# Keys in runs, scores at a step, and the banks of P·V, relu and output dealt out anew: a fused window attention and MLP kernel

## The chip, the cores and the metric

The kernel runs on one core of one Trainium2 chip. The metric is the device time of one execution in microseconds (us). TensorE is called PE, VectorE DVE, ScalarE ACT, GpSimd POOL and SyncE SP; SP only issues DMAs here.

## The reference

Sliding window attention for 8 batches of 8 heads, 576 positions and 64 numbers a head, and then an MLP without residual on the 4608 rows of 512 that come out of it:

```python
scores = scale * np.matmul(q, k.transpose(0, 1, 3, 2))
mask = np.abs(pos[:, None] - pos[None, :]) <= 32
attn = softmax(np.where(mask, scores, -1e9))           # with + 1e-9 in the divisor
x = np.matmul(attn, v)  ->  transposed to (B*S, H*D) = (4608, 512)
r = np.maximum(x @ w_in, 0.0)                          # w_in 512 x 2048
out = (s * (r * r) + b) @ w_out                        # w_out 2048 x 512, s and b scalars
```

All inputs and the output are float32. The kernel computes its matmuls in bf16.

## The kernel before

The 4608 rows are 36 tiles of 128 tokens. A tile is two units of 64 queries; with a window of 32, each unit needs 128 keys, which overlap by half, so a tile needs 192 keys (32 before it to 32 behind it). All eight heads of a tile are done together, as four pairs of heads.

**Order.** Nothing is looped over in the finished program. Each operation is added as a node with an engine, a cost, a key and the names it reads and writes; `_Plan.order` then simulates the engines with these costs and takes, on whichever engine comes free, the ready node with the smallest key. The outcome is a fixed instruction list for each engine, with semaphore waits between them. Keys count tokens: the FFN of a tile has the key of its tokens (`t0`), its attention is drawn ahead by `akey(j) = 128*j - min(640, 500 + 50*j)`. An engine may be given as a set, such as `("act", "dve")`; the planner then chooses. Nodes marked `small` use the PE array as quarters of 64 x 64, and the planner tries to keep them together (`HOLD`, `DEFER`), since a switch costs time. `fill` puts idle matmuls on PE ahead of a node for which the plan waits, in the stages named by `FILL`, in number by `FILL_SHARE` and `FILL_NS`.

**Attention.** Loads of q, k and v go through SP's queue in order (`load`, L506), each gated by the tile five before it. POOL casts them to bf16 (`cast_kq`, `cast_v`). From tile 12 on, DMA transposes q and k; up to 11, PE does it through the bank `TPF`. k is loaded as two neighbouring token rows in one partition, so that after the transposition the even and the odd keys lie in two halves, 1 KB apart; `scores` (L798) reads them in the order of tokens:

```python
kk = KQT["k"][...][rows, :, pr, p0 % 128:p0 % 128 + (x1 - x0) // 2].rearrange("q t p -> q p t")
```

The first four tiles take keys and queries from `TURN` (`kwt`, `qwt`), which the first batch's raw rows are turned into on PE (`turn_raw`), and there the keys lie in runs. Scores fill two PSUM banks `SC`. DVE adds the mask and takes the maximum (L810), ACT exponentiates (L818), POOL divides (L831). From tile 6 on a DMA transposes the probabilities into `PTS` (L845).

**P·V.** `VE[j]` holds the 128 rows of v that begin 32 before the tile, so unit 0 has its keys in `VE[j]` and unit 1 has half in `VE[j]`, half in `VE[j+1]`. Up to `NOLD` (6), unit 1 has its own copy `VO` in key order (`make_vo`, two casts of 64 rows), and `av_one` (L869) does 16 matmuls in full-array mode into the bank `AV`. From `NOLD` on, `av` (L886, L892) does 24 matmuls in quarter mode, into `AV` and a second bank, `PTPF`; ACT copies the second bank (`HALF`, L901), and DVE adds the two into `XT` (L903). Tiles 0 to 2 (`LIGHT`) go another way: `attend_light` computes the scores a second time in transposed form and does P·V in two steps of 16 and 8 matmuls (L733).

**FFN.** The first 8 tiles run alone, the other 28 in pairs of 256 tokens. `s1` (L992) multiplies `XT` by w_in into a relu bank, ACT takes the relu (L1001), DVE squares it (L1020), `s2` (L1040) multiplies by w_out, and DVE scales and adds a constant row into `OUTS` (L1054), from which SP stores. Of the eight PSUM banks, the relu banks are `HT[0]`, `HT[1]` and, from token 1408 on, `TPF`; the out bank is `OUTP`, and for tiles 0 to 4 `PTPF` in turn with it (`ONE`). The last three pairs turn through four banks.

**Weights.** w_in and w_out come in four blocks each (`load_w`), as float32 into free parts of `GT` (`SLOT`), and are cast on POOL. The third and the fourth w_out block reuse the slots of the first and the second.

Of the kernel before, what the change touches and what calls it, by code (L numbers as in the profile page):

```python
# [6 lines left out]
F32 = mybir.dt.float32  # L7
# [7 lines left out]
DM = H * D  # L15
# [12 lines left out]
FILL, FILL_MIN, FILL_SHARE, FILL_NS = ("attn", "ffn", "sums"), 300.0, 0.7, 115.0  # L28
# [34 lines left out]
class _Plan:  # L63
# [202 lines left out]
    last = {}  # L266
# [4 lines left out]
def bass_sliding_window_symmetric__then__act_starrelu_kernel(  # L271
# [19 lines left out]
    WSET = {"i": ("pool",), "o": ("pool",)}  # L291
# [3 lines left out]
    SLOT = dict(i0=0, i1=1, i2=2, i3=3, o0=2, o1=3, o2=2, o3=3)  # L295
# [5 lines left out]
    NWHOLE = 0  # L301
    AVK, NOLD, ONE, NVO = 5, 6, 5, 2
# [11 lines left out]
    def OSET(j):  # L314
        return ("act", "dve")

    with ExitStack() as es:
# [31 lines left out]
        OUTS = [sb((128, DM), F32, "outs") for _ in range(NO)]  # L349
# [28 lines left out]
        AVF = ps((128, 512), F32, "av")  # L378
        AV = AVF[:, :].rearrange("p (a b) -> p a b", b=128)
# [66 lines left out]
        def fill(e, stage, n):  # L446
            for _ in range(n):
                if stage == "sums":
                    r = e.matmul(OUTP[:, 0:256], lhsT=NIL[:, :], rhs=ONES[:, :], start=False,
                                 stop=False)  # L450
                else:
                    r = e.matmul((HT[1] if stage == "attn" else OUTP)[:, 0:256],
                                 lhsT=ONES[:, 0:128], rhs=ONES[:, :], start=True, stop=True)
# [17 lines left out]
        def load_w(which, c):  # L471
            s_ = SLOT[which + str(c)]
            w32 = GT[:, 4 + 2 * s_:6 + 2 * s_, :, :].rearrange("p a b c -> p (a b c)").bitcast(
                F32).rearrange("p (g c) -> p g c", g=4)
            src = (w_in[:, :, 512 * c:512 * c + 512] if which == "i"
                   else w_out[:, 4 * c:4 * c + 4, :])
            lastload[0] = add("sp", lambda e: [e.dma_start(w32, src)], 500, -LEAD - 900,
                              writes=[("W32", s_, g) for g in range(4)], dsem=f"dw{s_}",
                              dtime=2850, behind=lastload[0], ndesc=512)
# [136 lines left out]
        def make_vo(j):  # L616
            s_, a, b_ = j % NVO, j % NVE, (j + 1) % NVE
            if j < LIGHT or j >= NOLD:
                return
            for r0, x in ((64, j), (0, j + 1)):  # L620
                sl = x % (NL + 1)
                move(OSET(j), {"act": 620.0, "dve": 425.0},
                     VO[s_][r0:r0 + 64, :], V32[sl][r0:r0 + 64, :],
                     akey(j) - 10, [("V32", sl)] + ([("V32", 0, "lo")] if x == 0 else []),
                     [("VO", s_, r0)])
# [30 lines left out]
        def attend_light(j):  # L656
# [69 lines left out]
            ve, vb = j % NVE, (j + 1) % NVE  # L726
            steps = [[(1, vb, 0, 64), (0, ve, 0, 128)], [(1, ve, 64, 128)]]
            before = None
            for i, step in enumerate(steps):
                def av(e, step=step, i=i):  # L730
                    for u, vt, k0, k1 in step:
                        for y in range(8):
                            r = e.matmul(AVF[64 * u:64 * u + 64, 64 * y:64 * y + 64],  # L733
                                         lhsT=PTS[ptb][k0:k1, y, 64 * u:64 * u + 64],
                                         rhs=VE[vt][k0:k1, 64 * y:64 * y + 64],
                                         start=(i == 0 and y == 0),
                                         stop=(y == 7 and (i == 1 or u == 0)))
                    return r

                n = add("pe", av, 300 * len(step), key + 3, reads=pts + [("VE", ve), ("VE", vb)],  # L740
                        writes=["AV"])
                n.hard, before = before, n
            turned[j] = n
# [29 lines left out]
        def attend(j):  # L773
# [12 lines left out]
            def scores(e):  # L786
                for pr in range(NPAIR):
                    for u, x0, x1, y0 in ((0, 0, 128, 0), (1, 0, 64, 128), (1, 64, 128, 64)):
                        for hh in range(2):
                            if whole:  # L790
                                qq, kk = qs(j, pr, hh, 64 * u, 64 * u + 64), keys(j, pr, hh, y0, y0 + x1 - x0)
                            else:
                                rows, p0 = slice(64 * hh, 64 * hh + 64), 64 * (j % 2) + y0 // 2
                                qq = KQT["q"][c % NKT["q"]][rows, j % 2, pr, 64 * u:64 * u + 64]
                                kk = KQT["k"][(c + p0 // 128) % NKT["k"]][
                                    rows, :, pr, p0 % 128:p0 % 128 + (x1 - x0) // 2].rearrange(
                                    "q t p -> q p t")
                            r = e.matmul(SC[hh][64 * u:64 * u + 64, pr, x0:x1], lhsT=qq, rhs=kk,  # L798
                                         start=True, stop=True)
                return r  # L800
# [81 lines left out]
            def av(e):  # L882
                for pr in range(NPAIR):
                    for hh in range(2):
                        d0, y = 128 * pr + 64 * hh, 2 * pr + hh
                        e.matmul(PTPF[64 * hh:64 * hh + 64, 128 * pr:128 * pr + 128],  # L886
# [12 lines left out]
            add("pe", av, 265, key + AVK, reads=pts + [("VE", ve), ("VE", (j + 1) % NVE)], writes=["AV", "PTP"]).mode = "small"  # L899
            hb = j % 2  # L900
            add("act", lambda e: e.copy(HALF[hb][:, :], PTPF[:, :]), 620, key + AVK, reads=["PTP"],  # L901
# [69 lines left out]
        for m, nt in enumerate(TILES):  # L971
# [8 lines left out]
            for f0 in range(0, 16, fg):  # L980
                hb, rb = hcnt[0] % (3 if KQDMA < NT and t0 >= 128 * KQDMA else 2), rcnt[0] % NR1
# [43 lines left out]
            for sub in range(nt // 128):  # L1025
                r0 = t0 + 128 * sub
                end = r0 + 128 == T
                for c0, cn in ((0, 256), (256, 256)) if end else ((0, 512),):
# [4 lines left out]
                                 )[ocnt[0] % (4 if last else 2 if t0 < 128 * ONE else 1)]  # L1033
# [17 lines left out]
                    if not cvec_done[0]:  # L1051
# [5 lines left out]
                        60 + 1.35 * cn, key - 2000, reads=[ores, "CVEC", "SCB"], writes=[("OUTS", ob)])  # L1057
# [63 lines left out]
```

## Time and profile before

| | before |
|---|---|
| median of 3 runs | 331.92 us (330.61 to 332.28) |
| the profiled execution | 331.01 us, span 329.3 us |
| granted TensorE clock, mean | 0.995 |
| busy: PE, DVE, ACT, POOL | 314.1, 219.6, 215.9, 163.1 us |
| scores L798 / P·V L886 + L892 | 768 + 24 / 240 + 480 matmuls |
| idle fill matmuls L452 | 55, the last group at 24.10 us |

The profile comes from one execution. Busy time is the union of an engine's instructions; matmuls overlap, so the mean length of one is longer than the distance between two. In timelines each row is a start, a length, an engine, a line, an operation with output and inputs, its shape and count, and in brackets the idle time ahead of it.

### The profile page before, as it was taken

What the parts mean: (1) busy time and instruction counts of PE and PEld (TensorE: products, weight loads), DVE (VectorE), ACT (ScalarE), POOL (GpSimd) and SP (SyncE); (2) the same over time, 40 slices, a digit from 0 to 9 for tenths busy, and PEclk for the clock granted to TensorE, in tenths of its full rate; (3) what the DMA queues carried; (4) which work ended last, traced back from release to release, by engine and by line L of the source; (5) the groups of instructions that cost most, each with busy time, mean ns of one, the idle gap of its engine ahead of it and who ended that gap; (6) DMA issues with size and microseconds to landing.
All of it is one profiled execution on the core that took longest, in us unless ns stands there. A gap on an engine that the chain in (4) does not pass through costs nothing.

```text
span 329.3 us, 10479 instructions
## 1 busy us (share of the span) xinstructions
PE 314.1 (95%) x4119; PEld 220.5 (67%) x4169; DVE 219.6 (67%) x869; ACT 215.9 (66%) x731; POOL 163.1 (50%) x220
## 2 busy tenths in 40 slices
PE   6889999999999999999999999999999999999996
PEld 4557966677776766766666676666767676656664
DVE  2446797888876887777667667767866767634332
ACT  5415745587877787697777777786877779723230
POOL 5576688565763656535454547464654532220000
PEclk9799999999999999999999999999999999999999
DMA  5999969939999999979999999999999652221011
GB/s 164 353 293 286 311 228 237 238 106 233 167 196 212 267 203 218 218 152 230 198 225 181 197 221 227 200 184 220 185 217 198 137 124 67 64 66 64 34 55 73
DMA packets 155297, 61.30 MB, mean 186 GB/s; under 512 B 129392, under 2 KB 146160, under 8 KB 155248
## 3 DMA queue, kind: packets, MB, share of 16 engines
q1 hardware_dynamic: 154960, 60.64, 87.1%
q8 instruction: 32, 0.52, 0.7%
q14 instruction: 17, 0.14, 0.2%
q10 hardware_dynamic: 288, 0.00, 0.0%
HBM read 37.03 MB, written 9.44 MB: 141 GB/s over the span
## 4 chain that ended last, share of the span: by engine, by line
PE 79%; DMA 9%; DVE 3%; POOL 3%; issue 3%; SPq 2%; POOLq 0%
PE outp L1040 26%; PE ht L992 25%; PE tp L992 8%; PE sc L798 5%; DMA gt<-in_q_dram 3%; DMA v<-in_v_dram 2%; PE sc L1040 2%; DMA pts<-p 2%; DMA r32k<-in_k_dram 2%; PE ptp L886 2%; PE ptp L1040 2%; PE av L1040 2%; DVE gt L1020 1%; SPq L506 1%; POOL p L831 1%
## 5 line engine op out<-in xcount | busy, mean ns | idle before, releaser
L1020 DVE TENSOR_TENSOR gt<-r 128x512 bf16<-128x512 bf16 x144 | 82.4, 574 | 54.8 <-ACT r L1001 53.5
L831 POOL TENSOR_TENSOR p<-p,rc 128x512 bf16<-128x512 bf16 x65 | 72.6, 1136 | 90.0 <-DVE rc L826 90.0
L1040 PE MATMUL outp<-wout,gt 128*128 128x512 bf16 (+1 forms) x436 | 111.9, 375 | 5.1 <-issue 4.1
L992 PE MATMUL ht<-xt,win 128*128 128x256 bf16 (+1 forms) x1152 | 114.1, 249 | 0.8 <-DVE xt L903 0.4
L818 ACT ACTIVATE p<-ss,mx 128x128 bf16<-128x128 f32 x264 | 103.0, 392 | 17.8 <-DVE mx L810 17.5
L992 PEld LDWEIGHTS ht<-xt,win 128*128 128x128 bf16 x1152 | 91.9, 98 | 24.8 <-DVE xt L903 1.2
L1001 ACT ACTIVATE r<-ht 128x512 bf16<-128x512 f32 x112 | 66.2, 592 | 44.4 <-PE ht L992 43.6
L810 DVE CUSTOM_DVE_ANT_0 ss<-sc,mask 128x128 f32<-128x128 f32 x264 | 62.1, 282 | 12.6 <-PE sc L798 12.3
L1040 PEld LDWEIGHTS outp<-wout,gt 128*128 128x128 bf16 x480 | 43.4, 98 | 33.8 <-issue 0.4
L818 ACT ACTIVATION_READ_ACCUMULATOR p<-ss,mx 128x1 f32 x264 | 50.0, 189 | 0.0
L992 PE MATMUL tp<-xt,win 128*128 128x256 bf16 x256 | 33.2, 273 | 0.0
L992 PEld LDWEIGHTS tp<-xt,win 128*128 128x128 bf16 x256 | 25.0, 98 | 8.0
L526 POOL CAST ve<-v 128x512 bf16<-128x512 f32 x37 | 24.0, 653 | 11.7 <-PE av L892 9.7
L1001 ACT ACTIVATE r<-tp 128x512 bf16<-128x512 f32 x32 | 18.9, 592 | 12.3 <-PE tp L992 11.1
L526 POOL CAST kn<-r32k 128x512 bf16<-128x512 f32 x34 | 21.5, 659 | 7.3 <-DMA r32k<-in_k_dram 7.3
L1054 DVE SCALAR_TENSOR_TENSOR outs<-outp,scb,cvec 128x512 f32<-128x512 f32 (+1 forms) x30 | 22.1, 736 | 3.4 <-PE outp L1040 3.4
L901 ACT COPY half<-ptp 128x512 f32<-128x512 f32 x30 | 17.4, 579 | 10.5 <-PE av L892 10.5
L526 POOL CAST qn<-r32q 128x512 bf16<-128x512 f32 x32 | 20.1, 628 | 4.2 <-DMA r32q<-in_q_dram 4.2
L798 PE MATMUL sc<-kt,qt 64*64 64x64 bf16 (+1 forms) x768 | 22.1, 243 | 0.0
L810 DVE DVE_READ_ACCUMULATOR2_ANT mx<- 128x1 f32 x264 | 21.3, 81 | 0.0
L903 DVE TENSOR_TENSOR xt<-av,half 128x512 bf16<-128x512 f32 x30 | 20.5, 683 | 1.1 <-ACT half L901 1.1
L798 PEld LDWEIGHTS sc<-kt,qt 64*64 64x64 bf16 x768 | 17.5, 107 | 4.7 <-issue 3.6
(133 smaller groups left out, 244.2 us busy)
## 6 DMA issues: line engine op xcount, KB each, us to landing
out_dram<-outs SPq DMA_DIRECT2D x35, 256.0 KB, 3.1
v<-in_v_dram SPq DMA_DIRECT2D x28, 256.0 KB, 5.5
r32q<-in_q_dram SPq DMA_DIRECT2D x28, 256.0 KB, 4.9
r32k<-in_k_dram SPq DMA_DIRECT2D x9, 512.0 KB, 5.0
gt<-in_moe_w_in_dram SPq DMA_DIRECT2D x4, 1024.0 KB, 10.0
gt<-in_moe_w_out_dram SPq DMA_DIRECT2D x4, 1024.0 KB, 6.9
v<-in_v_dram SPq DMA_DIRECT2D x8, 192.0 KB, 4.7
r32k<-in_k_dram SPq DMA_DIRECT2D x3, 448.0 KB, 4.5
```

The costliest lines, as they stand in the source:

```text
L526: return e.tensor_copy(dst, src)
L798: r = e.matmul(SC[hh][64 * u:64 * u + 64, pr, x0:x1], lhsT=qq, rhs=kk, start=True, stop=True)
L810: lambda e, ss=ss, x=x, y=y, pr=pr, hh=hh: e.tensor_tensor_reduce(out=SS[ss][:, x, :], in0=SC[hh][:, pr, :], in1=MASK[kind][:, :], scale=- ...
L818: lambda e, ss=ss, x=x, y=y: e.activation(P[pb][:, y, :], SS[ss][:, x, :], AF.Exp, bias=MX[mb][:, y:y + 1], scale=-1.0, accum_out=SM[mb][: ...
L831: return e.tensor_tensor(P[pb][:, y0:y0 + 4, :], P[pb][:, y0:y0 + 4, :], RC[mb][:, y0:y0 + 4].unsqueeze(2).broadcast_to([128, 4, 128]), AL ...
L901: add("act", lambda e: e.copy(HALF[hb][:, :], PTPF[:, :]), 620, key + AVK, reads=["PTP"], writes=[("HALF", hb)])
L903: add("dve", lambda e: e.tensor_tensor(XT[:, :, 128 * (j % NX):128 * (j % NX) + 128], AV[:, :, :], HALF[hb][:, :].rearrange("p (a b) -> p ...
L992: r = e.matmul(hbank[:, nt * f:nt * f + nt], lhsT=WIN[:, kc, 128 * ft:128 * ft + 128], rhs=XT[:, kc, x0:x0 + nt], start=(kc == 0), stop=(k ...
L1001: return e.activation(R1[rb][:, :], hbank[:, :], AF.Relu, bias=0.0, scale=1.0)
L1020: return e.tensor_tensor(d, r, r, ALU.mult)
L1040: r = e.matmul(op_[:, 0:cn], lhsT=GT[:, g_, fc, :], rhs=WOUT[:, fc, c0:c0 + cn], start=(fc == 0), stop=(fc == 15))
L1054: add("dve", lambda e, ob=ob, op_=op_, c0=c0, cn=cn: e.scalar_tensor_tensor(OUTS[ob][:, 0:cn], op_[:, 0:cn], SCB[:, 0:1], CVEC[:, c0:c0 + cn],
```

## The change

- The keys of tiles 4 and on are read in two runs (even tokens, odd tokens), and the score matmul writes its columns at a step of two, so that the scores lie in token order as before.
- The second bank of P·V is `TPF` instead of `PTPF`. The relu banks are two throughout, and `OUTP` and `PTPF` take turns as out banks throughout.
- `AVK` goes from 5 to 384: P·V of tile j and the copy of its second bank get the key of the scores of tile j + 3.
- `NOLD` goes from 6 to 12, and the light tiles use `VO` too: their P·V is one step of 16 matmuls. The casts into `VO` may run on POOL for tiles 0 to 2.
- The third w_out block is staged in the four output buffers (now one tensor), the fourth in the third's old slot; w_out is cast on ACT or POOL.
- Fillers are 512 columns wide, planned as half of waits over 400 ns, and not in the stage "ffn". The planner is given longer times for the first raw loads.

```diff
-FILL, FILL_MIN, FILL_SHARE, FILL_NS = ("attn", "ffn", "sums"), 300.0, 0.7, 115.0
+FILL, FILL_MIN, FILL_SHARE, FILL_NS = ("attn", "sums"), 400.0, 0.5, 220.0
...
-    WSET = {"i": ("pool",), "o": ("pool",)}
+    WSET = {"i": ("pool",), "o": ("act", "pool")}
...
-    SLOT = dict(i0=0, i1=1, i2=2, i3=3, o0=2, o1=3, o2=2, o3=3)
+    SLOT = dict(i0=0, i1=1, i2=2, i3=3, o0=2, o1=3, o2=4, o3=2)
...
-    NWHOLE = 0
-    AVK, NOLD, ONE, NVO = 5, 6, 5, 2
+    NWHOLE, SECOND = 0, True
+    AVK, NOLD, ONE, NVO = 384, 12, 11, 2
...
     def OSET(j):
-        return ("act", "dve")
+        return ANY if j < LIGHT else ("act", "dve")
...
-        OUTS = [sb((128, DM), F32, "outs") for _ in range(NO)]
+        OUTA = sb((128, NO, DM), F32, "outs")
+        OUTS = [OUTA[:, i, :] for i in range(NO)]
...
+        AV2, AV2N = (TPF, "TP") if SECOND else (PTPF, "PTP")
...
-        add("pe", lambda e: fill(e, "attn", 14), 2990, K0, reads=["ONES", "NIL"]).tag = "attn"
+        add("pe", lambda e: fill(e, "attn", 7), 2990, K0, reads=["ONES", "NIL"]).tag = "attn"
...
-            w32 = GT[:, 4 + 2 * s_:6 + 2 * s_, :, :].rearrange("p a b c -> p (a b c)").bitcast(
-                F32).rearrange("p (g c) -> p g c", g=4)
+            w32 = OUTA if s_ == 4 else GT[:, 4 + 2 * s_:6 + 2 * s_, :, :].rearrange(
+                "p a b c -> p (a b c)").bitcast(F32).rearrange("p (g c) -> p g c", g=4)
...
-                              dsem=f"dr{x}{half}", dtime=1500, behind=lastload[0], ndesc=128)
+                              dsem=f"dr{x}{half}", dtime=1900 if x + str(half) != "K0" else 2650, behind=lastload[0], ndesc=128)
...
-            if j < LIGHT or j >= NOLD:
+            if j >= NOLD:
                 return
...
-            steps = [[(1, vb, 0, 64), (0, ve, 0, 128)], [(1, ve, 64, 128)]]
...
+            def av(e):
+                for u, vt in ((0, VE[ve]), (1, VO[vo])):
+                    for y in range(8):
+                        r = e.matmul(AVF[64 * u:64 * u + 64, 64 * y:64 * y + 64],
+                                     lhsT=PTS[ptb][:, y, 64 * u:64 * u + 64],
+                                     rhs=vt[:, 64 * y:64 * y + 64], start=(y == 0), stop=(y == 7))
+                return r
...
+                            dst = SC[hh][64 * u:64 * u + 64, pr, x0:x1]
...
                                 kk = KQT["k"][(c + p0 // 128) % NKT["k"]][
-                                    rows, :, pr, p0 % 128:p0 % 128 + (x1 - x0) // 2].rearrange(
-                                    "q t p -> q p t")
-                            r = e.matmul(SC[hh][64 * u:64 * u + 64, pr, x0:x1], lhsT=qq, rhs=kk,
-                                         start=True, stop=True)
+                                    rows, :, pr, p0 % 128:p0 % 128 + (x1 - x0) // 2]
+                                dst = dst.rearrange("q (p t) -> q t p", t=2)
+                            r = e.matmul(dst, lhsT=qq, rhs=kk, start=True, stop=True)
...
-                        e.matmul(PTPF[64 * hh:64 * hh + 64, 128 * pr:128 * pr + 128],
+                        e.matmul(AV2[64 * hh:64 * hh + 64, 128 * pr:128 * pr + 128],
...
-                hb, rb = hcnt[0] % (3 if KQDMA < NT and t0 >= 128 * KQDMA else 2), rcnt[0] % NR1
+                hb, rb = hcnt[0] % (3 if not SECOND and t0 >= 128 * KQDMA else 2), rcnt[0] % NR1
...
-                                 )[ocnt[0] % (4 if last else 2 if t0 < 128 * ONE else 1)]
+                                 )[ocnt[0] % (4 if last else 2 if SECOND or t0 < 128 * ONE else 1)]
...
-                        60 + 1.35 * cn, key - 2000, reads=[ores, "CVEC", "SCB"], writes=[("OUTS", ob)])
+                        60 + 1.35 * cn, key - 2000, reads=[ores, "CVEC", "SCB"], writes=[("OUTS", ob), ("W32", 4, ob)])
```

More of the change, by code (lines that the diff above doesn't have):

```diff
@@ L621, in make_vo @@
                 sl = x % (NL + 1)
-                move(OSET(j), {"act": 620.0, "dve": 425.0},
+                move(OSET(j), {"act": 620.0, "dve": 425.0, "pool": 640.0},
                      VO[s_][r0:r0 + 64, :], V32[sl][r0:r0 + 64, :],
@@ L725, in attend_light @@
             pts = [("PTS", ptb, y) for y in range(8)]
-            ve, vb = j % NVE, (j + 1) % NVE
-            steps = [[(1, vb, 0, 64), (0, ve, 0, 128)], [(1, ve, 64, 128)]]
[L728 to L743, printed above, removed]
+            ve = j % NVE
+            vo = j % NVO
+            def av(e):
[5 more added lines that the diff above has]
+                return r
+            turned[j] = add("pe", av, 700, key + 3,
+                            reads=pts + [("VE", ve), ("VO", vo, 0), ("VO", vo, 64)], writes=["AV"])
             def rows(e):
```

13 lines of the change are left out of this document (6 added, 7 removed).

## The prediction

> **What bounds the kernel now.** I read the page first: the busy table, the row of 40 slices, the chain that ended last.
>
> ```profile
> span 329.3 us, 10479 instructions
> ...
> PE 314.1 (95%) x4119; PEld 220.5 (67%) x4169; DVE 219.6 (67%) x869; ACT 215.9 (66%) x731; POOL 163.1 (50%) x220
> ...
> PE   6889999999999999999999999999999999999996
> ...
> PE 79%; DMA 9%; DVE 3%; POOL 3%; issue 3%; SPq 2%; POOLq 0%
> ```
>
> TensorE (PE) is busy in 95% of the span and carries 79% of the chain; no other engine passes 67%. Then the windows, one for each stage: the light start, the time until w_out is in, the stage with two relu banks, the stage with three, the end.
>
> ```profile
> 14.90:26.48 11.58, 10.18 (x205) 6.35 (x205) 4.65 (x12) 2.37 (x5) 7.96 (x14) 1.00 0.98 325
> 26.48:60.00 33.52, 32.42 (x539) 25.59 (x537) 27.07 (x75) 18.65 (x55) 24.36 (x37) 1.00 1.00 254
> 60.00:115.00 55.00, 53.69 (x835) 38.97 (x847) 43.62 (x192) 42.42 (x159) 32.52 (x43) 1.00 1.01 203
> 135.00:282.00 147.00, 143.47 (x1783) 100.31 (x1804) 105.05 (x457) 112.72 (x400) 75.22 (x93) 1.00 0.98 183
> 282.00:329.30 47.30, 44.13 (x372) 28.60 (x376) 18.11 (x49) 15.62 (x37) 2.90 (x3) 1.00 0.19 62
> ```
>
> The columns are length, then busy time with its count for PE, PEld, DVE, ACT and POOL, then the granted clock (1.00 in all of them), DMA share and GB/s. From 26.48 us, where the first tile's FFN begins, PE lacks 1.10, 1.31 and 3.53 us, which is 2 to 3%. Part of that is not idleness: where a group of four matmuls shows three records, the missing one is counted as a 0.16 us gap (a row below). So from 26.5 us on the time is the sum of what PE is given to do. An edit that takes matmul time away shortens the kernel by that much, and an edit that only removes waits of other engines brings next to nothing.
>
> **The change part by part.** *Scores.* All 32 full-form tiles from 4 on read keys at L798 in steps of 1 KB (two interleaved token rows); tile 3 reads the same shapes in runs, from the turned first batch.
>
> ```profile
> L798 PE MATMUL sc<-kt,qt 64*64 64x64 bf16 x512 | 22.0, 222 | 0.0
> L798 PE MATMUL sc<-kt,qt 64*64 64x128 bf16 x256 | 21.8, 284 | 0.0
> ...
> L798 PE MATMUL sc<-kwt,qwt 64*64 64x64 bf16 x16 | 0.4, 195 | 0.0
> L798 PE MATMUL sc<-kwt,qwt 64*64 64x128 bf16 x8 | 0.4, 222 | 0.0
> ```
>
> One 128-column matmul takes 284 ns with the step and 222 in runs, one of 64 columns 222 against 195: 62 and 27 ns more. Of a whole block the timeline gives the cost, as the distance to the next group on PE:
>
> ```profile
> 31.99 0.45 PE L798 MATMUL sc<-kwt,qwt 64*64 64x128 bf16 x24
> 32.37 1.01 PE L992 MATMUL ht<-xt,win 128*128 128x128 bf16 x15
> ...
> 62.19 0.69 PE L798 MATMUL sc<-kt,qt 64*64 64x128 bf16 x24
> 62.81 1.04 PE L1040 MATMUL outp<-wout,gt 128*128 128x512 bf16 x4
> ```
>
> 24 matmuls take 0.38 us in runs and 0.62 with the step. After the change all 32 blocks read runs: 32 x 0.24 = 7.7 us off, if the new step of two fp32 elements in the score bank is free. No row of the trace shows a matmul that writes with a step. Its bounds: the write can't be better than in runs, so 0.38 us is the floor; the nearest row above is the stepped read, 0.62, where nothing is gained. I take 0.38, because the rows that differ here differ in the read alone, and no row shows PE held by its writes. [...]
>
> *P·V of tiles 12 to 35, tied to the scores three tiles on.* These blocks switch PE into quarter-array mode and back, as the scores do.
>
> ```profile
> 122.24 0.24 PE L886 MATMUL ptp<-pts,ve 64*64 64x128 bf16 x2
> ...
> 183.25 0.24 PE L886 MATMUL ptp<-pts,ve 64*64 64x128 bf16 x2
> ...
> 183.50 0.28 PE L798 MATMUL sc<-kt,qt 64*64 64x128 bf16 x1
> ...
> 184.35 0.81 PE L1040 MATMUL outp<-wout,gt 128*128 128x512 bf16 x3 [0.16 <-issue]
> ...
> 197.38 0.69 PE L798 MATMUL sc<-kt,qt 64*64 64x128 bf16 x24
> 198.22 0.81 PE L1040 MATMUL outp<-wout,gt 128*128 128x512 bf16 x3 [0.16 <-issue]
> 198.97 0.24 PE L886 MATMUL ptp<-pts,ve 64*64 64x128 bf16 x2
> ...
> 199.34 0.82 PE L1040 MATMUL outp<-wout,gt 128*128 128x512 bf16 x3
> ...
> 245.59 0.24 PE L886 MATMUL ptp<-pts,ve 64*64 64x128 bf16 x2
> ```
>
> The record left out before 184.35 and 198.22 is one of about 0.22 us (four last 1.04 in a row above, three 0.81), so those groups begin at 184.13 and 198.00. Together the pair takes 184.13 - 183.25 = 0.88 us. Apart they take 0.62 + 0.37 = 0.99, and each stands behind a switch of some 0.10 (198.00 + 4 x 0.22 = 198.87, and the block begins at 198.97): 0.2 us more. In the trace the P·V of six tiles from 12 on stands apart (the first at 122.24, the last before the scores run out at 245.59), and after it one more of the last three does, because tiles 33 to 35 find no scores three tiles on: five pairs saved, 1.0 us. The key also puts the copy of the second bank on ScalarE (L901) later, behind relus. What covers that: the key lets P·V run 256 tokens before its FFN, two tiles, and 36 tiles take some 300 us, 8.3 each. If the cover failed, that copy and the add (0.58 and 0.68 us, below) would be late on PE.
>
> *Tiles 6 to 11 by the older form.* They take the one-bank form of P·V (L869), which tiles 3 to 5 show:
>
> ```profile
> 59.09 0.32 PE L869 MATMUL av<-pts,ve 128*64 128x64 bf16 x8
> ...
> 59.47 0.62 PE L642 MATMUL tp<-ident,kn 128*128 128x128 bf16 x8
> ```
>
> That is 59.47 - 59.09 = 0.38 us in full-array mode, against 0.25 (183.50 - 183.25) for the quarter form where it is paired and 0.37 plus a switch of 0.10 where it isn't. With four of the six paired: 4 x 0.13 - 2 x 0.09 = +0.3 us. Each also needs two casts into VO on ScalarE or VectorE, and loses the copy of the second bank:
>
> ```profile
> L901 ACT COPY half<-ptp 128x512 f32<-128x512 f32 x30 | 17.4, 579 | 10.5 <-PE av L892 10.5
> L531 ACT CAST vo<-v 64x512 bf16<-64x512 f32 x2 | 1.2, 614 | 0.5 <-PE av L869 0.4
> ...
> L903 DVE TENSOR_TENSOR xt<-av,half 128x512 bf16<-128x512 f32 x30 | 20.5, 683 | 1.1 <-ACT half L901 1.1
> L526 DVE CAST vo<-v 64x512 bf16<-64x512 f32 x4 | 3.2, 806 | 1.0 <-DMA v<-in_v_dram 1.0
> ```
>
> Twelve casts at the mean of 614 and 806, less six copies of 579: 8.5 - 3.5 = 5.0 us more on two engines that have 11.4 and 12.6 us free of 55 in that stage. Hidden, it costs nothing; behind each cast wait exponentials (ACT) or squares (DVE) in line, and these feed PE. Bounds 0 and 5.0; I take 1.0, near the end that PE's 2% of idleness in the stage speaks for.
>
> *Light tiles 0 to 2.* Their P·V goes from 24 matmuls in two steps, the second waiting for the first, to 16 of the form of L869; six VO casts are added on whichever engine is free (ACT 2.37 and DVE 4.65 us of 11.58 busy).
>
> ```profile
> 22.08 0.80 PE L733 MATMUL av<-ve,pts 64*64 64x64 bf16 x16
> 22.81 0.39 PE L691 MATMUL ptp<-maskt,ident 128*128 128x512 bf16 x1
> ...
> 23.61 0.41 PE L733 MATMUL av<-ve,pts 64*64 64x64 bf16 x8
> 23.95 0.22 PE L704 MATMUL sc<-ident,m 128*16 128x128 bf16 x1
> 24.10 0.77 PE L452 MATMUL ht<-ones 128*128 128x256 bf16 x4
> ...
> 26.48 1.07 PE L992 MATMUL ht<-xt,win 128*128 128x128 bf16 x16
> ```
>
> 0.73 + 0.34 = 1.07 us become 0.38: 0.69 off each. For tiles 1 and 2, after 26.48, PE is full: 1.4 us off. For tile 0 the second step stood behind the next tile's scores, so its result came at 23.95 and could come at 22.08 + 0.38 = 22.46; PE's own work falls by 0.69 and the first FFN could begin up to 1.5 us earlier. I take 1.0.
>
> *Banks.* Relu banks go from three to two, out banks from one to two. The stage from 60 to 115 us already runs on two relu banks and one out bank, with PE 97.6% busy, like the stage with three (97.6%): nothing either way. The stepped write fills the same places, so readers of the scores see no change.
>
> *w_out, fillers, dtimes.* The third w_out load no longer waits on SP's queue for POOL's casts, and those casts may go to ScalarE:
>
> ```profile
> SPq L477 <- POOL wout L526: 8.8, 2, 5.4
> ```
>
> Loads of q, k and v behind it come up to 5.4 us earlier. But PE lacks only 1.10 us between 26.48 and 60, covered by FFN work on the first tiles: at most 1.1 is to be had, and a cast in front of an exponential can lose as much; I take nothing. The fillers (L452) stand in predicted waits before 26.48 us; shorter ones could at most give back those like the 0.77 us at 24.10 or lose that in a colder clock; nothing again. The new dtimes only move the plan of the first casts.
>
> The sum: -7.7 - 1.0 + 0.3 + 1.0 - 1.4 - 1.0 = -9.8 us. The profiled execution took 331.01 us with 329.3 of span; 331.0 - 9.8 = 321.2. The median of the runs shown is 0.9 above the profiled one, so I forecast **322.1 us**, and 319.5 to 325 if its mechanism holds.
>
> **The rivals.** *The step only moves from the read to the write.* The write costs what the read cost, the blocks stay at 0.62 us, and the rest remains: -9.8 + 7.7 = -2.1, 329.8 us. For it: the halved rate of the read at a step shows that this engine's streams can be held by a step. Against it: no row shows PE waiting on its bank. [...]
>
> *Slower: the stepped write costs more than the stepped read.* Its place is the 32 blocks at L798. If the write adds to the old block once more what the step added to the read, a block takes 0.62 + 0.24 = 0.86 us: 32 x 0.24 - 2.1 = +5.6, 337.5 us. It decides from (2.1 + 1.7) / 32 = 0.12 us above the old block, at 0.74 us. For it: all four quarters of the array write at once, two of them into one bank. Against it: a read at 62 ns extra for 128 columns is a rate of one half, and nothing suggests a quarter.
>
> *The other engines become the bound in tiles 6 to 11.* All 5.0 us of added casts come out on PE instead of 1.0: 326.1 us. For it:
>
> ```profile
> 70.00:80.00 10.00, 9.79 (x161) 7.27 (x161) 9.41 (x45) 7.78 (x33) 6.26 (x8) 1.00 0.61 146
> ```
>
> DVE is busy 9.41 of 10 us there. Against it: PE is full in that same window.
>
> **How the numbers follow.** Forecast 0.52; other engines bound 0.10; step moved to the write 0.22; slower 0.16. About 0.5% (1.7 us) is what a measurement of this kernel tells from no change. The first two are faster; the third, at 329.8, lies just past that bound, and I give 0.13 of it to faster and 0.09 to the same. Faster 0.75, same 0.09, slower 0.16. The range 319.5 to 331.0 holds the first three cases and leaves out the slower one and a few hundredths below.
>
> **What would show it.** In the new profile: the L798 forms at 222 and 195 ns, a block at 0.38 us before a full-array group, P·V of tile j right beside the scores of tile j + 3, L733 with 16 matmuls in 0.4 us, the first FFN near 25.5 us, and PE still above 97% in the middle stages. Wrong: L798 at 284 ns or more, or PE's share falling in 60 to 115 us while DVE or ACT rises above 90%.

## The result, and the profile after

| | before | changed |
|---|---|---|
| median, first comparison | 332.1 us (4 runs) | 327.57 us (4 runs), ratio 0.986 [0.982, 0.991] |
| median, once more beside the experiments | 331.17 us (11 runs) | 325.64 us (4 runs), ratio 0.982 [0.980, 0.985] |
| profiled execution | 331.01 us, span 329.3 | 326.15 us, span 324.4 |

The change makes the kernel 4.5 to 5.5 us faster. The forecast was 9.8 us, to 322.1: the direction and the outer range (319.5 to 331.0) hold, but less than half of the gain came, in the first comparison. The experiments below compare by ratios to the kernel before, each on the chip that it ran on; 0.1% is 0.33 us.

The page of the changed kernel, its busy table, slices and chain:

```profile
span 324.4 us, 10296 instructions
...
PE 308.5 (95%) x4013; PEld 215.3 (66%) x4064; DVE 218.3 (67%) x878; ACT 223.0 (69%) x742; POOL 157.3 (49%) x212
...
PE   6689989999999999999999999999999999999996
...
PE 78%; DMA 10%; DVE 3%; POOL 3%; SPq 2%; issue 2%; ACT 1%; DVEq 0%; POOLq 0%
```

The same stages as before (length, then busy time of PE, PEld, DVE, ACT, POOL, granted clock, DMA share, GB/s):

```profile
14.90:26.48 11.58, 10.39 (x224) 6.25 (x222) 7.55 (x19) 3.70 (x8) 8.10 (x14) 1.00 0.98 331
26.48:60.00 33.52, 31.32 (x513) 24.44 (x516) 25.89 (x79) 21.62 (x60) 20.76 (x31) 1.00 1.10 269
60.00:115.00 55.00, 53.33 (x774) 38.76 (x779) 45.69 (x207) 46.28 (x172) 33.48 (x41) 1.00 1.05 201
135.00:282.00 147.00, 144.89 (x1810) 101.07 (x1833) 102.82 (x463) 114.53 (x403) 72.34 (x90) 1.00 0.98 184
```

PE is still the bound: it lacks 1.67 and 2.11 us in the two long stages, 1.31 and 3.53 before. What is new is idleness between 26.48 and 60 us, 2.20 us against 1.10. PE's busy time as a whole fell by only 5.6 us. Where the rest was to come from, the groups of the score matmuls and a block in the timeline show:

```profile
L795 PE MATMUL sc<-kt,qt 64*64 64x64 bf16 x512 | 20.3, 242 | 0.0
L795 PE MATMUL sc<-kt,qt 64*64 64x128 bf16 x256 | 20.0, 306 | 0.0
...
63.24 0.64 PE L795 MATMUL sc<-kt,qt 64*64 64x128 bf16 x24
63.81 1.07 PE L988 MATMUL ht<-xt,win 128*128 128x128 bf16 x16
```

Single matmuls did not fall to 195 and 222 ns, as the shapes that run on do, but stand at 242 and 306, above before's 222 and 284. Matmuls overlap (24 of them, 242 or 306 ns long, in 0.57 us), so the distance from a block to the next group tells more than the length of one: a block takes 0.57 us (63.24 to 63.81), where before took 0.62 and the forecast had 0.38. The start of the FFN, and the light P·V:

```profile
20.53 0.34 PE L733 MATMUL av<-ve,pts 128*64 128x64 bf16 x5
...
21.06 0.39 PE L692 MATMUL ptp<-maskt,ident 128*128 128x512 bf16 x1
...
24.48 1.07 PE L988 MATMUL ht<-xt,win 128*128 128x128 bf16 x16
```

The light P·V takes 0.53 us in one step (0.38 forecast, 1.07 before), and the first FFN begins 2.0 us earlier than before (1.5 us earlier in a second profile of the same kernel, e0, where it begins at 25.02).

### The profile page after: what moved, and what is told of

Its sections match the earlier page's. It is cut to its first block, busy times and chain, and to the rows that moved or that the text cites. A ratio compares the mean times of both kernels' runs of the same rounds, so it can differ in the third digit from the quotient of the medians.

```text
span 324.4 us, 10296 instructions
## 1 busy us (share of the span) xinstructions
PE 308.5 (95%) x4013; PEld 215.3 (66%) x4064; DVE 218.3 (67%) x878; ACT 223.0 (69%) x742; POOL 157.3 (49%) x212
## 4 chain that ended last, share of the span: by engine, by line
PE 78%; DMA 10%; DVE 3%; POOL 3%; SPq 2%; issue 2%; ACT 1%; DVEq 0%; POOLq 0%
PE ht L988 35%; PE outp L1036 16%; PE ptp L1036 15%; PE sc L795 5%; DMA gt<-in_moe_w_out_dram 3%; DMA gt<-in_q_dram 3%; DMA gt<-in_moe_w_in_dram 3%; PE sc L1036 2%; DMA r32k<-in_k_dram 2%; SPq L507 2%; PE av L1036 2%; PE tp L882 1%; DVE gt L1016 1%; PE av L888 1%; POOL win L527 1%
## 5 line engine op out<-in xcount | busy, mean ns | idle before, releaser
L988 PE MATMUL ht<-xt,win 128*128 128x256 bf16 (+1 forms) x1408 | 147.4, 253 | 0.3 <-issue 0.3
L988 PEld LDWEIGHTS ht<-xt,win 128*128 128x128 bf16 x1408 | 116.4, 98 | 33.4 <-issue 0.5
L997 ACT ACTIVATE r<-ht 128x512 bf16<-128x512 f32 x144 | 85.3, 594 | 52.3 <-PE ht L988 50.2
L1036 PE MATMUL outp<-wout,gt 128*128 128x512 bf16 (+1 forms) x243 | 62.7, 372 | 3.7 <-issue 1.7
L1036 PE MATMUL ptp<-wout,gt 128*128 128x512 bf16 x237 | 61.6, 379 | 1.7 <-issue 1.0
L1036 PEld LDWEIGHTS outp<-wout,gt 128*128 128x128 bf16 x272 | 24.9, 98 | 19.1 <-ACT wout L532 0.5
L1036 PEld LDWEIGHTS ptp<-wout,gt 128*128 128x128 bf16 x256 | 24.1, 98 | 18.3
L527 POOL CAST kn<-r32k 128x512 bf16<-128x512 f32 x34 | 21.8, 670 | 9.3 <-DMA r32k<-in_k_dram 9.3
L897 ACT COPY half<-tp 128x512 f32<-128x512 f32 x24 | 14.0, 583 | 12.7 <-PE av L888 12.7
L899 DVE TENSOR_TENSOR xt<-av,half 128x512 bf16<-128x512 f32 x24 | 16.2, 676 | 0.9 <-ACT half L897 0.8
L1050 DVE SCALAR_TENSOR_TENSOR outs<-outp,scb,cvec 128x512 f32<-128x512 f32 (+1 forms) x17 | 12.4, 727 | 1.1 <-PE outp L1036 1.1
L527 POOL CAST win<-gt 128x512 bf16<-128x512 f32 x16 | 10.0, 664 | 4.8 <-DMA gt<-in_moe_w_in_dram 4.8
```

Of the source, the lines that this page charges most:

```text
L527: return e.tensor_copy(dst, src)
L897: add("act", lambda e: e.copy(HALF[hb][:, :], AV2[:, :]), 620, key + AVK, reads=[AV2N], writes=[("HALF", hb)])
L899: add("dve", lambda e: e.tensor_tensor(XT[:, :, 128 * (j % NX):128 * (j % NX) + 128], AV[:, :, :], HALF[hb][:, :].rearrange("p (a b) -> p ...
L988: r = e.matmul(hbank[:, nt * f:nt * f + nt], lhsT=WIN[:, kc, 128 * ft:128 * ft + 128], rhs=XT[:, kc, x0:x0 + nt], start=(kc == 0), stop=(k ...
L997: return e.activation(R1[rb][:, :], hbank[:, :], AF.Relu, bias=0.0, scale=1.0)
L1036: r = e.matmul(op_[:, 0:cn], lhsT=GT[:, g_, fc, :], rhs=WOUT[:, fc, c0:c0 + cn], start=(fc == 0), stop=(fc == 15))
```

## The experiments

Theory A was formed on that trace: the step only moved from the read to the write, which holds the matmul nearly as much. Its rival, theory B, was the forecast's: the write is free, and the gain was lost elsewhere.

**The score matmuls alone, in both kernels, and without any step**

e1 gives the kernel before the new score matmuls only; e2 takes them out of the changed kernel:

```diff
# e1, on the kernel before            # e2 is the reverse, on the changed kernel
-  kk = KQT["k"][...][rows, :, pr, ...].rearrange("q t p -> q p t")
+  kk = KQT["k"][...][rows, :, pr, ...]
+  dst = dst.rearrange("q (p t) -> q t p", t=2)
```

> The kernel before, with the score matmuls alone changed: keys read in runs, scores written at a step of two. The order of all work is that of before. Theory A (a step of two fp32 in the PSUM write holds the matmul nearly as much as the 1 KB step in the read): a score block takes 0.57 us where before took 0.62, so 32 x 0.05 = 1.6 us less than before, some 330.5 us, ratio 0.995. Theory B (the forecast's: the write is free, and what after lost it lost elsewhere): a block 0.38 us, 7.7 us less, 324.4 us, ratio 0.977.

330.05 us, ratio 0.997 [0.995, 0.999]: 1.1 us less, blocks of 0.57 us, and PE's work in the order of before.

> The changed kernel, with the score matmuls alone put back: keys read at the 1 KB step, scores written in runs. Theory A: a block 0.62 us, 1.6 us more than the changed kernel's 327.6, so 329.2, and still 2.9 us under before from the other parts. Theory B: 7.7 us more than the changed kernel, 335.3, which is slower than before, so the other parts would have cost 3.

327.77 us, ratio 0.990 [0.987, 0.992], blocks of 0.62 us: the rest of the change is worth 3.5 us, and the score matmuls the 2.4 us between this and the changed kernel (0.982, in the second comparison; by the first, 0.986, they would be worth 1.0). Theory B's numbers (324.4 and 335.3) are excluded by both.

e3 leaves no step anywhere:

```diff
-  dst = dst.rearrange("q (p t) -> q t p", t=2)
+  dst = dst.rearrange("q (t p) -> q t p", t=2)
```

> The changed kernel, with keys read in two runs and scores written in runs too, so that even keys' scores lie ahead of the odd ones and the mask and v meet them in the wrong order: the part left out is the putting in order. Same instructions in the same order. Theory A: the 306 and 242 ns of the two forms fall to 222 and 195, a block to 0.38 us, and 32 x 0.19 = 6.1 us come off: 321.5. Theory B (two runs 1 KB apart, or four quarters at once, are what holds the block): 0.57 us stays, 327.6.

321.14 us, ratio 0.968 [0.965, 0.970]. The same instructions in the same order, and the groups read:

```profile
L795 PE MATMUL sc<-kt,qt 64*64 64x64 bf16 x512 | 14.0, 195 | 0.0
L795 PE MATMUL sc<-kt,qt 64*64 64x128 bf16 x256 | 13.2, 222 | 0.0
```

The block is 0.38 us, and 4.9 us come off (0.982 - 0.968), most of the 32 x 0.19 = 6.1. So two runs 1 KB apart cost nothing to read; what is left in the changed kernel is the write.

**What in the write it is**

e5 writes two neighbouring columns at a time and then jumps; e6 steps in both streams:

```diff
# e5
-  kk = KQT["k"][...][rows, :, pr, ...]
-  dst = dst.rearrange("q (p t) -> q t p", t=2)
+  kk = KQT["k"][...][rows, :, pr, ...].rearrange("q t (a c) -> q t a c", c=2)
+  dst = dst.rearrange("q (a b c) -> q b a c", b=2, c=2)
# e6
+  kk = KQT["k"][...][rows, :, pr, ...].rearrange("q t p -> q p t")
+  dst = dst.rearrange("q (t p) -> q p t", t=2)
```

> The changed kernel, keys read in runs, scores written in pairs: two neighbouring columns, then on by four. The columns come out in another order than the mask's, so the putting in order is left out; the instructions and their order are those of the changed kernel. [...] If any break in the write holds it: a block near 0.57 us, 327 us.

> The changed kernel, keys read at the 1 KB step and scores written at a step of 64, so that neither stream runs on; scores come out in another order than the mask's (that is left out). If reading and writing are held side by side and the slower one sets the time: a block of 0.62 us, 328 us, as with the read step alone. If the two costs add: 0.38 + 0.24 + 0.19 = 0.81 us, 32 x 0.19 = 6 us more, 334 us.

One run each, 321.77 and 328.11 us. First the groups of e5, with pairs, then those of e6, with both steps:

```profile
L796 PE MATMUL sc<-kt,qt 64*64 64x64 bf16 x512 | 14.1, 195 | 0.0
L796 PE MATMUL sc<-kt,qt 64*64 64x128 bf16 x256 | 13.2, 222 | 0.0
```

```profile
L796 PE MATMUL sc<-kt,qt 64*64 64x64 bf16 x512 | 21.9, 224 | 0.0
L796 PE MATMUL sc<-kt,qt 64*64 64x128 bf16 x256 | 21.6, 287 | 0.0
```

Pairs are as fast as a run, 222 ns. Both steps together take what the read step alone took, 287 ns against 284 in before, and the two groups are busy for 21.9 and 21.6 us, against 22.0 and 21.8, so the two steps don't add here. That reading and writing go side by side, and the slower one sets the time, fits this but is not shown: e6 writes at a step of 64 columns, not of two, and that write was not run by itself. What is shown is 306 ns for single columns at a step of two against 222 for pairs, so not every break in the write holds it.

**Keys in token order: a version that beats both**

e4 loads k as q is loaded, one token a partition, so that after the transposition keys lie in token order and neither stream needs a step. e11 is e4 with k's loads planned at the old time; e17 gives the same to the kernel before.

```diff
-  load("k", 256 * c - 32, 256, 2, R32["k"][s_], ("R32", "k", s_, 0), ...)
+  for t in range(2):
+      load("k", 256 * c - 32 + 128 * t, 128, 1, R32["k"][s_][:, DM * t:DM * t + DM], ("R32", "k", s_, t), ...)
...
-  kk = KQT["k"][...][rows, :, pr, p0 % 128:p0 % 128 + (x1 - x0) // 2]
+  kk = KQT["k"][...][rows, t_, pr, p0 % 128:p0 % 128 + x1 - x0]
# e11 besides
-  dtime=(1300.0 if row == 1 else 900.0) * tot / 128
+  dtime=(1300.0 if x != "k" else 900.0) * tot / 128
```

> The changed kernel, with k loaded and transposed one token a partition, as q is, so that keys lie in token order: read in one run, written in a run, nothing reordered. k then moves in pieces of 256 B instead of 512, 18 chunk loads become 36. Theory A: blocks of 0.38 us, 6.1 us off, 321.5 us, if the DMA engines (89% busy) carry the shorter pieces. If they don't: the loads land late, PE waits for k or for the transposed probabilities, and some or all of the 6.1 us is lost again. Theory B: no change, 327.6.

323.72 us, ratio 0.977 [0.974, 0.979]. Blocks of 0.38 us, yet 2.6 us above e3 on the same chip, with PE busy all through:

```profile
135.00:282.00 147.00, 147.00 (x1840) 98.16 (x1840) 108.46 (x474) 113.72 (x416) 75.06 (x92) 1.00 1.02 193
```

So PE did not wait for the DMAs. PE's list is another one: quarter-mode blocks from tile 4 on (scores and two-bank P·V standing alone or together) number 49, against 36 in e3 and in the changed kernel. 13 switches for 2.6 us would be 0.2 us each, the forecast's price.

> The version with k one token a partition, read and written in runs (323.7 us), with one planner figure more: k's loads planned at 900 ns for 128 tokens as before, not 1300. In the earlier run the planner, expecting k later, split 16 of the 24 pairs of scores and P.V; here PE's list is that of the changed kernel again, with all its pairs. Theory (2.6 us of that version were 13 or so mode switches of 0.2 us): 321.2 us, PE full from 60 us on. Rival (the shorter DMA pieces cost it): it stays at 323.7 us or goes above, with PE idle where k lands late.

322.04 us, ratio 0.971 [0.968, 0.974], with 36 blocks and the changed kernel's order again. That is 1.9 us less than e4 (0.977 - 0.971), some 0.15 us for each of the 13 switches; the 1.1 us that are left above e3 (0.971 - 0.968) lie within the uncertainty and are not located. It is 9.1 us faster than before and 3.6 us faster than the changed kernel on the same chip.

> The kernel before with k loaded and transposed one token a partition (planned at the old load time), so that keys are read and scores written in runs, all else as before, PE's list too. The forecast's first term, 32 x 0.24 = 7.7 us, is what a score block without any step is worth: 323.6 us, ratio 0.977, blocks of 0.38 us. Rival (PE's time saved is taken back by waits elsewhere, so that the term would have been too large even with a free write): 326 us or more, with PE idle.

328.56 us, ratio 0.993 [0.991, 0.995]: 2.4 us, not 7.7, though the score matmuls are down to 219 and 194 ns. The time saved was taken back, as the rival said. But the expectation's condition, PE's list of before, did not hold: the list differs in 15 places between 68 and 160 us (before has its first two-bank P·V and a score block together at 80.48 us, e17 has them apart at 82.22 and 83.56). PE's waits between 60 and 135 us, from the timeline:

```profile
61.88 0.62 PE L640 MATMUL tp<-ident,qn 128*128 128x128 bf16 x8 [0.31 <-POOL qn L526]
71.23 0.62 PE L640 MATMUL tp<-ident,qn 128*128 128x128 bf16 x8 [1.22 <-POOL qn L526]
100.11 0.24 PE L884 MATMUL ptp<-pts,ve 64*64 64x128 bf16 x2 [0.47 <-DMA pts<-p]
108.47 0.24 PE L884 MATMUL ptp<-pts,ve 64*64 64x128 bf16 x2 [0.59 <-DMA pts<-p]
115.20 0.24 PE L884 MATMUL ptp<-pts,ve 64*64 64x128 bf16 x2 [0.33 <-DMA pts<-p]
121.29 0.45 PE L796 MATMUL sc<-kt,qt 64*64 64x128 bf16 x24 [1.19 <-DMA qt<-qn]
```

They add to 4.1 us that the kernel before does not have (0.2 us for `pts` in all). PE now waits for casts and DMA transposes. Whether the shorter pieces of k (1.11 DMA share from 60 to 115 us, 1.01 before), the other order or the faster PE makes them late, this run doesn't tell; the changed kernel with the same loads (e4, e11) has next to none of these waits.

**The other parts, each put back in the changed kernel**

> The changed kernel once more, for a narrower interval beside the others: 0.986 of before, 326.8 to 327.6 us, blocks of 0.57 us.

325.64 us, ratio 0.982 [0.980, 0.985]; this is what the following are held against.

```diff
# e7
-    AVK, NOLD, ONE, NVO = 384, 12, 11, 2
+    AVK, NOLD, ONE, NVO = 5, 12, 11, 2
```

> The changed kernel with AVK back at 5: P.V of a tile as soon as it is ready, not with the scores three tiles on. By the forecast the tie saves 0.2 us for each pair that stood apart, five pairs, so 1.0 us more than the changed kernel. Rival (the tie does nothing, since the planner pairs them anyway by HOLD): within 0.3 us of the changed kernel.

327.27 us, 0.987 [0.985, 0.989]: 1.6 us more. But PE's list has 37 quarter-mode blocks instead of 36, so without the tie the planner still pairs all but one of the blocks that the tie pairs, much as the rival said, and pairing is worth some 0.2 us of it; the rest isn't located.

e8 gives tiles 0 to 2 their two steps from `VE` again, and `make_vo` returns for `j < LIGHT`.

> The changed kernel with the light tiles' P.V back in two steps of 16 and 8 matmuls, and no VO casts for them. By the forecast: 2.4 us more than the changed kernel, the first FFN again near 26.5 us instead of 24.5. By the new trace (a step of 16 takes 0.53 us, not 0.38): 0.54 x 2 + 2.0 = 3.1 us more at most. Rival (the time to the first FFN is made up later, because PE then waits for w_out at 37 us): under 1 us more.

326.27 us, 0.984 [0.982, 0.986]: 0.6 us more, which isn't clear of none. The first FFN still begins early:

```profile
24.81 1.07 PE L993 MATMUL ht<-xt,win 128*128 128x128 bf16 x16
```

So the light P·V did not bring that. What did stands in before's own trace, which I had read as a share of the chain ("issue") and not followed up:

```profile
18.02 0.21 PE L696 MATMUL ptp<-qwt,kwt 64*64 64x128 bf16 x1 [1.40 <-issue]
```

In the middle of the first transposed scores PE stands for 1.4 us and waits for nothing that the profile shows. e12 puts the fillers and load times back into the changed kernel, e15 puts the new ones into the kernel before:

```diff
# e15, on the kernel before (e12 is the reverse, on the changed kernel, without the stage "ffn")
-FILL, FILL_MIN, FILL_SHARE, FILL_NS = ("attn", "ffn", "sums"), 300.0, 0.7, 115.0
+FILL, FILL_MIN, FILL_SHARE, FILL_NS = ("attn", "sums"), 400.0, 0.5, 220.0
...  # 512 columns, 7 instead of 14 at the start, load times 1900 and 2650 for 1500
```

> The changed kernel with the fillers as before (256 columns, 0.7 of waits over 0.3 us) and the old load times in the planner. In before's trace PE stood 1.4 us in the middle of the first transposed scores (L696, at 16.6 us) with nothing to wait for that the profile shows; before with new score matmuls shows the same stop at the same matmul, and no kernel with the new fillers does. Theory C (the stop belongs to a place in PE's list: after some 220 matmuls, which the fewer, wider fillers move behind the scores into a wait): here 210 matmuls stand ahead of these scores again, as in before, against 192 in the changed kernel; the stop returns, the first FFN begins near 26 us instead of 24.5 to 25.0, and the kernel is 1 to 1.5 us slower than the changed one. Rival (the earlier first FFN comes from the light tiles' shorter P.V, as forecast): first FFN stays at 25 us, no stop, within 0.5 us of the changed kernel.

> The kernel before with the new fillers and the new load times alone. Theory C: 192 matmuls ahead of the first transposed scores, no stop, first FFN near 25 us, 1 to 1.5 us less than before (ratio 0.996). Rival (the light tiles' P.V brought it): first FFN at 26.5 us, ratio 1.000.

e12: 326.41 us, 0.985 [0.984, 0.987], 1.0 us more. e15: 330.26 us, 0.998 [0.996, 0.999], 0.8 us less than before. First e12's stop, its first FFN and a second stop, then e15's first FFN, with no stop before it:

```profile
17.75 0.21 PE L698 MATMUL ptp<-qwt,kwt 64*64 64x128 bf16 x1 [1.34 <-issue]
...
25.56 1.07 PE L989 MATMUL ht<-xt,win 128*128 128x128 bf16 x16
...
30.79 0.40 PE L989 MATMUL ht<-xt,win 128*128 128x128 bf16 x4 [0.38 <-issue]
```

```profile
24.88 1.07 PE L991 MATMUL ht<-xt,win 128*128 128x128 bf16 x16
```

The stop goes and comes with the fillers and load times, which these runs change together. It stands at one place in PE's list: in all four kernels that show it, behind 437 recorded matmuls and weight loads (218 of them matmuls). In the kernels with the new fillers that place holds a matmul that waits for DVE anyway, so the place is not gone but covered. A second such place lies 512 records on, behind 949: there e12 stands for 0.38 us (30.79 above), and e16, a run of the next section, for 1.47. First the covered place in the changed kernel, then e16:

```profile
17.91 0.22 PE L705 MATMUL sc<-ident,m 128*16 128x128 bf16 x1 [0.75 <-DVE m L686]
```

```profile
32.66 0.56 PE L988 MATMUL ht<-xt,win 128*128 128x128 bf16 x7 [1.47 <-issue]
```

e12 and e15 have a third, behind 1205 and 1203 records (0.75 and 0.71 us). The pages of both kernels also have a row that was not followed up; here it is the changed kernel's:

```profile
q8 instruction: 32, 0.52, 0.7%
```

That queue moves 32 packets of kind "instruction", one for about 252 of the 8077 matmuls and weight loads on the page. The stops are some 512 and 256 instructions apart. My estimate from these counts alone is that PE stood for its own program to be loaded; no run shows it.

```diff
# e10
-    WSET = {"i": ("pool",), "o": ("act", "pool")}
+    WSET = {"i": ("pool",), "o": ("pool",)}
-    SLOT = dict(i0=0, i1=1, i2=2, i3=3, o0=2, o1=3, o2=4, o3=2)
+    SLOT = dict(i0=0, i1=1, i2=2, i3=3, o0=2, o1=3, o2=2, o3=3)
```

> The changed kernel with w_out staged and cast as before (third and fourth block in the first two's slots, POOL alone). By the forecast: the same, at most 1.1 us either way. Rival (with the first FFN 2 us earlier PE now waits for w_out, 1.3 us of idle time at 37 to 42 us, and the old staging is later still): 1 to 3 us more, PE idle at L1036 between 37 and 56 us.

327.96 us, 0.989 [0.987, 0.991]: 2.2 us more. Not by the rival's way: PE's idle time from 26.48 to 60 us is 2.04 us, no more than the changed kernel's 2.20. But the planner's list came out with 43 quarter-mode blocks instead of 36: seven switches, 1.0 to 1.4 us at 0.15 to 0.2 each. So the staging seems to have acted in part, about half of it, through the order; the rest is not located.

**The banks, and tiles 6 to 11**

```diff
# e9
-    NWHOLE, SECOND = 0, True
+    NWHOLE, SECOND = 0, False
# e13 besides: AVK 384 -> 5.    e16 instead: ONE 11 -> 8.
# e14, on the changed kernel: NOLD 12 -> 6
```

> The changed kernel with the banks dealt as before from tile 11 on: three relu banks, P.V's second bank PTPF, one out bank; NOLD and AVK as changed. By the forecast: the same within 0.5 us. Rival (two out banks or two relu banks matter, since PE now has less other work to put between): over 1 us either way, with PE idle at L1036 or L988.

337.5 us, 1.018 [1.015, 1.020]: slower than before. The loss has one place, in the timeline (first three rows) and in the windows of 10 us:

```profile
135.59 0.24 PE L882 MATMUL ptp<-pts,ve 64*64 64x128 bf16 x2 [1.05 <-DVE outs L1050]
138.18 0.24 PE L882 MATMUL ptp<-pts,ve 64*64 64x128 bf16 x2 [1.53 <-DVE xt L899]
140.49 0.32 PE L882 MATMUL ptp<-pts,ve 64*64 64x128 bf16 x2 [1.86 <-DVE xt L899]
```

```profile
130.00:140.00 10.00, 5.89 (x113) 3.19 (x112) 6.17 (x39) 6.37 (x29) 6.69 (x9) 0.97 0.89 188
140.00:150.00 10.00, 9.51 (x83) 7.59 (x84) 4.21 (x10) 5.42 (x15) 5.02 (x7) 0.68 1.12 204
```

Three P·V blocks stand in a row, the first waiting for the bank's output to be drained, the next two for the P·V before; from 140 to 150 us the granted clock is 0.68 in the mean. The next 24 matmuls of 256 columns on PE take 5.09 us there (141.07 to 146.16), 0.21 us each, where before's take 0.11 (eight from 186.74 to 187.61). The expectation of e13 has 3.4 us at half clock; a mean of 0.68 over 10 us is 6.4 us at a half, by estimate.

> The changed kernel with both the banks back (three relu banks, PTPF as second bank of P.V, one out bank) and AVK back at 5. With the banks alone put back it took 337.5 us: PE stood 4 us at 130 to 141 us, where PTPF goes over from output to P.V, and then ran 3.4 us at half clock. Theory D (the banks are free by themselves; what cost 11 us is the late P.V together with a second bank that output shares up to there, so that several late P.V blocks stand in a row, each waiting for the one before to be drained): with early P.V the stop goes, and the time is that of the changed kernel with AVK 5, 327.3 us, within 1 us. Rival (the banks by themselves cost it): 335 us or more.

335.57 us, 1.012 [1.010, 1.014]. Theory D falls: early P·V doesn't help, and PE again waits 3.4 us at L882 for L899. In program order the output of tile 11 still goes through `PTPF` just ahead of P·V of tile 12, so that P·V can't run ahead there, whatever its key.

> The changed kernel with the banks back (AVK stays 384), and ONE 8 instead of 11: output leaves PTPF after tile 7, four tiles before P.V takes it over as second bank at tile 12. With ONE 11 the output of tile 11 was still named for PTPF just ahead of P.V of tile 12, and PE stood there, with AVK 5 as well. Theory E (the stop was that handover, and the banks are otherwise free, as forecast): no stop at 130 to 145 us, 325.6 to 327.5 us, the changed kernel's time within 1 us. Rival (three relu banks and one out bank cost it by themselves in this kernel): 335 us or more.

330.6 us, 0.995 [0.993, 0.998]: the stop at 130 us is gone, so the handover had caused it. But 4.3 us remain against the changed kernel, so theory E doesn't hold whole. Its list has 40 quarter-mode blocks (four switches, 0.6 to 0.8 us), and its stop at 32.66 us is about 1.1 us longer than that of the changed kernel at the same place (0.32). In the stage from 135 us on PE lacks 1.84 us, with 1.1 us of it one wait of the single out bank for its drain; but the changed kernel lacks 2.11 there, so this stage doesn't hold the loss:

```profile
135.00:282.00 147.00, 145.16 (x1813) 98.36 (x1812) 108.51 (x470) 113.70 (x413) 72.58 (x91) 1.00 1.01 190
...
PE outp L1036 <- DVE outs L1050: 1.1, 1, 1.1
```

In the profiled execution PE also ran at a granted clock of 0.57 from 20 to 24 us and near 0.8 from 32 to 40; how much of the median that is stays open.

> The changed kernel with NOLD back at 6: tiles 6 to 11 do P.V in quarter mode again with two banks, without the two VO casts. By the forecast NOLD 12 cost 0.3 us on PE and an allowance of 1.0 for the casts, so 1.3 us less than the changed kernel. Rival (the casts are hidden, and the second bank TPF collides with the transposes of k and q that go through it up to tile 11): 0 to 3 us more, with PE waiting at L643 or L882 between 60 and 115 us.

375.2 us, 1.134 [1.132, 1.136], far outside both expectations. The waits of PE:

```profile
PE tp L882 <- DMA pts<-p: 19.8, 4, 9.4
PE sc L795 <- DVE mx L806: 8.3, 4, 2.1
PE tp L643 <- ACT half L897: 2.8, 4, 0.7
```

`TPF` also takes the transposes of k and q up to tile 11. The operations on a bank keep the order in which they were added, so the transposes of tile j + 1 now wait for P·V of tile j (the third row), and attention can't run ahead. These waits are 31 of the 50 us lost; the granted clock was low besides, 0.60 from 110 to 120 us and 0.50 from 120 to 130. NOLD 12 is a condition of the new second bank, not a term beside it; its cost by itself is not measured.

## Why the prediction was right or wrong

**Direction and bound: right.** PE stayed the bound in the changed kernel, and both comparisons give less time.

**Scores, -7.7 us: the step that failed.** They gave 1.1 us alone and 2.4 as the last part, 1.6 by 32 x 0.05 in the trace. The place was "I take 0.38, because the rows that differ here differ in the read alone, and no row shows PE held by its writes". No row of before writes at a step, so that absence said nothing; of the two bounds, 0.38 and 0.62, the blocks landed at 0.57. The first rival, the step that only moves, had the mechanism (its "halved rate" of the read is 62 ns for 64 columns more with the step, 27 in runs), and its 329.8 us is 2 to 4 above the result because the rest brought 3.5 us (e2), not 2.1, and the write's step costs a little less than the read's (0.57 us a block, not 0.62). It was given 0.22, and the runs speak for it: 128 columns written at a step of two took 306 ns, against 222 without a step (e3). But not every break in the write costs time, since pairs, which are not contiguous as a whole, stood at 222 (e5).

**The worth of a block without a step** was borne out in the changed kernel, where e3 took 4.9 of 6.1 us, and not in the kernel before, where e17 took 2.4 of 7.7, with another order and other loads besides. "An edit that takes matmul time away shortens the kernel by that much" holds while nothing else comes due; in e17 casts and DMA transposes did, for 4.1 us.

**P·V tied, -1.0.** 1.6 us measured, but one block more or less in the lists: sized by luck. In the changed kernel the planner pairs all but one of these blocks by itself (e7), so there were no five pairs to save. The price of a switch, 0.2 us, held roughly (0.15 by e4 against e11, 0.2 by e3 against e4).

**Light tiles, -2.4.** 0.6 measured, 0.5 us on PE for each (0.53, not 0.38, per block). The 1.0 us for tile 0 was a wrong cause: the first FFN came 1.5 to 2.0 us earlier, mainly by a stop of 1.3 to 1.5 us that the fillers and load times decide, and I had taken "nothing" for these. They were worth 0.8 to 1.0 us, and the colder clock that I had set against them did not come: granted 0.51 from 10.9 to 14.4 us before, 1.00 from 10 to 15 us in the changed kernel.

**w_out, nothing.** 2.2 us, about half of it by the switches in the planner's order, if their price holds there. The bound, PE's idle time of before, counted waits and not switches.

**Banks, nothing.** Not shown: no run with the old banks in the changed kernel kept everything else. The old banks at the handover cost 7 us (e9 against e16) to 8 us (e13 against e7).

**Tiles 6 to 11, +0.3 and 1.0 allowed.** Not separable. DVE and ACT stayed at 45.7 and 46.3 us of 55, and PE lacked 1.67 us there against 1.31 before, so the rival's 5.0 us on PE did not come.

The parts put back one at a time add to 2.4 + 1.6 + 0.6 + 1.0 + 2.2 = 7.8 us, against 5.5 to 5.9 for the whole; each carries an uncertainty of 0.5 to 1 us, and all act on one planned order.

## What to carry to other kernels

A stride that is moved from a matmul's input to its output need not be gone; here a block went from 0.62 us to 0.57, and to 0.38 with neither. Bound it by what a row shows for the other stream, and don't take missing rows as a free price. Look for the layout in which neither side needs it, here one token a partition for k, which gave 3.6 us more. Where a planner or scheduler orders the work, compare its lists too: a load time that looks neutral moved 13 mode switches (e4) and a staging buffer seven (e10), and e17 was no clean comparison because its order had changed.

## What the runs showed of the hardware that I had not expected

A matmul of 128 columns on a 64 x 64 quarter took 222 ns where both streams ran on, 284 with single elements read 1 KB apart, 306 with columns written at a step of two fp32, 222 with columns written in pairs, and 287 with both streams stepped (the write at a step of 64). PE stopped for 1.3 to 1.5 us behind 437 matmuls and weight loads, in four kernels with the narrow fillers, with nothing to wait for in the profile, and for 0.32 (the changed kernel) to 1.47 us (e16) behind 949. After waits of 4.4 us in all at 130 to 141 us the granted clock was 0.68 from 140 to 150 us.
